# Order of the first loads in a one-token attention and MLP kernel: K ahead of the query weights, three small loads behind a GpSimd mask

## The chip, the cores and the metric

The kernel runs on one core of one Trainium2 chip. The metric is the device time of one execution in microseconds (us). The core has a matrix engine (TensorE, PE in the profile), VectorE (DVE), ScalarE (ACT), GpSimd (POOL) and SyncE (SP), which here only issues transfers. Sixteen DMA engines move the data between the memory (DRAM) and the on-chip SBUF. Transfers that SP issues form one queue (q1 in the profile); those that ScalarE issues form another (q10).

## What is computed

The reference works on one token with 1024 features (bfloat16) and adds three terms:

```python
x  = A_x                                   # (1, 1, 1024)
xn = layernorm(x)
# attention over the last W = 4096 positions of a cache, 32 query heads, 4 KV heads, head size 128
q  = xn @ wq                               # wq (1024, 4096)
p  = softmax(q @ k.T * 128 ** -0.5)        # k, v: (4 heads, 4096, 128)
a  = (p @ v) @ wo                          # wo (4096, 1024)
# MLP with a layernorm of its own
h  = gelu(layernorm(xn) @ w1 + b1)         # w1 (1024, 3584)
m  = h @ w2 + b2                           # w2 (3584, 1024)
out = x + a + m
```

All weights and the cache window together are 39.85 MB, and each byte is used once.

## The kernel before

The kernel is one instruction stream for each engine, written out by hand, with semaphores between them. There is no loop over tiles of an activation: the work is a row of stages, and each stage consumes one large transfer.

**Transfers.** SP issues everything large, in this order: the first half of wq (4 MB, line 157, called from `load_chunks`), the first half of K (2 MB, line 231, `load_k`), the second half of wq (4 MB), the second half of K (2 MB), and w1 (7 MB). These five go out at the start with no wait. SP then waits for VectorE's fourth transpose of K (`C["kt", 3]`), issues V (2 x 2 MB, line 311) into the room of K, waits for the last query matmul and issues w2 (4 MB and 3 MB) into the room of wq, waits for the last matmul with w1 and issues wo in four pieces (16, 11, 4 and 1 of its 32 chunks, line 318). In K and V one row of a transfer is 16 KB, in the halves of wq 32 KB.

**Small loads.** ScalarE issues three small loads as its first instructions: x (2 KB in 16 rows of 128 B, line 166, `row_load`, semaphore `s_x`), b2 (the same form, `s_b2`) and b1 (7 KB in 32 rows of 224 B, line 170, `s_b1`). It then waits for GpSimd to have zeroed `QBD` (line 178), zeroes three PSUM banks (lines 223 and 224) and later computes the square roots of the layernorms (line 251).

**Constants.** GpSimd builds masks and zeroed tiles from 0.81 us on: `onesb` (line 175), `identb` (memset in line 177, made an identity by the affine select in line 180), `QBD`, `YZ`, `XZ`, and more up to line 219.

**The stages.** (1) TensorE spreads x over 128 partitions (line 426, waits for `s_x`), VectorE makes the two layernorms and the transposed x (lines 244 to 277, ending in `XZ`, line 274). (2) TensorE multiplies with wq (64 matmuls of the `add` helper, line 430; a register loop waits on `s_feed`, which GpSimd raises when a half of wq has landed). (3) Meanwhile VectorE transposes K in four pieces (`turn_k`, line 284); the first three stand in its program in front of the query's transpose (line 292), the fourth behind the copies into `QBD` (line 303). (4) TensorE computes the scores (32 matmuls), VectorE the maximum, ScalarE the exponentials (line 344). (5) TensorE multiplies with w1 (56 matmuls), then probabilities with V (32 matmuls). (6) TensorE multiplies with w2 and wo in 11 rounds of 8 matmuls, then with the last 16 chunks of wo in small tiles (line 507); both halves of the result are copied (line 400) and stored (line 402).

Since the `add` helper records every matmul under line 430, its stages are told apart by their tiles: XZ with BIG is the query stage, QBD with KT the scores, YZ with BIG the w1 stage, KT with KV the product with V, GO with BIG the last stage.

Of the kernel before, what the change touches and what calls it, by code (L numbers as in the profile page):

```python
# [19 lines left out]
NQ = HQ * DH  # L20
W1_CHUNKS = [8]
WQ_CHUNKS = [4, 4]
# [29 lines left out]
def bass_parallel_sum__sliding_block_cached__mixer_channel_mlp__decode_kernel(  # L52
# [17 lines left out]
    pe, dve, act, pool, sp = nc.tensor, nc.vector, nc.scalar, nc.gpsimd, nc.sync  # L70

    def sems(name, n):
        return [nc.alloc_semaphore(f"{name}{i}") for i in range(n)]

    s_x, s_b1, s_b2, s_v, s_out = (nc.alloc_semaphore(n) for n in ("s_x", "s_b1", "s_b2", "s_v", "s_out"))
    s_w1 = sems("s_w1", len(W1_CHUNKS))
    s_wq = sems("s_wq", len(WQ_CHUNKS))
# [6 lines left out]
    POOL = Track(nc, "S_POOL")  # L84
# [4 lines left out]
    def sb(name, shape, d):  # L89
        return nc.alloc_sbuf_tensor(name, shape, d)  # L90

    f32, bf16 = dt.float32, dt.bfloat16
    identb = sb("identb", [128, 128], bf16)
# [11 lines left out]
    B1R = sb("B1R", [32, F // 32], bf16)  # L105
# [32 lines left out]
    WA, W1 = BIG[:, 0:KC * NQ], BIG[:, KC * NQ:KC * NQ + KC * F]  # L138
# [8 lines left out]
    wq_p = A_wq.rearrange("(p r) n -> p r n", r=KC)  # L147
# [5 lines left out]
    C = {}  # L153

    def load_chunks(dst, src, chunks, width, semaphores, c0=0):
        for j, n in enumerate(chunks):
            sp.dma_start(  # L157
                dst[:, c0 * width:(c0 + n) * width].rearrange("p (c n) -> p c n", c=n),
                src[:, c0:c0 + n, :],
            ).then_inc(semaphores[j], 16)  # L160
            c0 += n

    XB = XBRP[:, :].rearrange("p (a n) -> p a n", a=16)[:, :, 0:D // 16]

    def row_load(dst, src, semaphore):
        act.dma_start(dst, src.rearrange("o (a n) -> o a n", a=16)).then_inc(semaphore, 16)

    row_load(XB[0:1], A_x.rearrange("b s n -> (b s) n"), s_x)
    row_load(XB[1:2], B_b2.rearrange("(o n) -> o n", o=1), s_b2)
    act.dma_start(B1R[:, :], B_b1.rearrange("(p c) -> p c", p=32)).then_inc(s_b1, 16)  # L170

    def pool_wait():
        pool.wait_ge(POOL.sem, POOL.cnt)

# [44 lines left out]
    POOL.mark(pool.tensor_tensor(out=HALF[:, :], in0=HALF4[:, 0:2], in1=HALF4[:, 2:4], op=ALU.add))  # L219
    C["consts"] = POOL.cnt  # L220

    act.wait_ge(POOL.sem, C["QBD"])
    ACT.mark(act.activation(out=PS[:, 0:1024], in_=QBD[:, :], func=ACTF.Copy))
    ACT.mark(act.activation(out=bank(7), in_=QBD[:, 0:512], func=ACTF.Copy))
# [5 lines left out]
    def load_k(c):  # L230
        sp.dma_start(KV[:, c * 8192:(c + 1) * 8192], pairs(A_k_cache, c)).then_inc(s_k[c], 16)  # L231

    load_chunks(WA, wq_p, WQ_CHUNKS[:1], NQ, s_wq)
    load_k(0)
    load_chunks(WA, wq_p, WQ_CHUNKS[1:], NQ, s_wq[1:], WQ_CHUNKS[0])
    load_k(1)
    load_chunks(W1, w1_p, W1_CHUNKS, F, s_w1)

# [321 lines left out]
```

## Time and profile before

| what | value |
|---|---|
| median of 3 runs | 98.8 us (98.8 to 98.97) |
| the profiled execution's own time | 99.37 us |
| its span, first to last instruction | 97.4 us |
| around the span | 1.97 us |
| TensorE busy | 73.0 us (75%) |
| VectorE, ScalarE, GpSimd busy | 38.9, 11.2, 9.9 us |
| moved by DMA | 39.88 MB, mean 409 GB/s over the span |
| packets of SP's queue, share of 16 engines' span | 95.7% |
| granted TensorE clock, mean | 0.965 |

The profile is of one execution, whose time is 0.57 us above the median of the runs without a profile, so sums are made against it and carried over as differences. "Busy" counts compute instructions alone; a transfer's issue takes an engine's sequencer (SPq, ACTq) but is not counted as busy. The chain that ended last follows the last instruction back to what released it, step by step.

### The profile page before, as it was taken

How to read it: one execution, taken by the hardware profiler on the slowest of the kernel's cores; microseconds unless marked ns; L12 is line 12 of the kernel's file. 1: busy time of each engine (PE TensorE's matmuls, PEld its weight loads, DVE VectorE, ACT ScalarE, POOL GpSimd, SP SyncE). 2: the span in 40 equal slices, each digit the busy share in tenths (PEclk: the TensorE clock that was granted, in tenths of full speed). 3: DMA queues.
4: the chain of work that ended last, by engine and by line, in shares of the span. 5: the costliest groups of instructions: out<-in, count | busy, mean ns of one | idle time of the engine just before them, and what ended most of it. 6: DMA issues, size and time to landing. Idle time of an engine off the chain costs nothing.

```text
span 97.4 us, 1285 instructions
## 1 busy us (share of the span) xinstructions
PE 73.0 (75%) x354; PEld 30.4 (31%) x354; DVE 38.9 (40%) x54; ACT 11.2 (12%) x20; POOL 9.9 (10%) x27
## 2 busy tenths in 40 slices
PE   0004000099999986999979999799999999779992
PEld 0000000033444431333434444333343443334450
DVE  0002899899930799940293620050048000000001
ACT  0880000600000024000005200200000000000001
POOL 6999400000000000000000000000000000000000
PEclk9999999999999998557999999999999999999999
DMA  7599999999999998888999999999999999899890
GB/s 215 256 431 431 405 432 444 431 444 431 410 431 481 636 424 377 377 377 377 437 431 431 437 498 431 431 444 394 394 464 498 431 431 431 376 435 426 372 377 1
DMA packets 1989, 39.88 MB, mean 409 GB/s; under 512 B 322, under 2 KB 324, under 8 KB 452
## 3 DMA queue, kind: packets, MB, share of 16 engines
q1 hardware_dynamic: 1876, 39.85, 95.7%
q10 hardware_dynamic: 112, 0.01, 0.1%
q8 instruction: 1, 0.02, 0.1%
HBM read 39.86 MB, written 0.00 MB: 409 GB/s over the span
## 4 chain that ended last, share of the span: by engine, by line
DMA 80%; PE 14%; SPq 3%; issue 1%; DVE 0%
DMA BIG<-in_B_w_dram 47%; DMA BIG<-in_A_wo_dram 33%; PE PS L430 13%; SPq L231 1%; SPq L157 1%; SPq L318 1%; DVE Pb L400 0%; PE PS L507 0%
## 5 line engine op out<-in xcount | busy, mean ns | idle before, releaser
L430 PE MATMUL PS<-BIG,XZ 128*128 x64 | 16.5, 427 | 10.2 <-DVE B L277 10.2
L430 PE MATMUL PS<-BIG,GO 128*128 (+1 forms) x148 | 22.2, 337 | 1.4 <-POOLq L420 1.2
L284 DVE STREAM_TRANSPOSE KT<-KV 128x4096 bf16<-128x4096 bf16 x4 | 17.6, 4432 | 4.8 <-DMA KV<-in_A_k_cache_dram 4.8
L430 PEld LDWEIGHTS PS<-BIG,GO 128*128 (+1 forms) x148 | 9.9, 97 | 13.8 <-issue 6.4
L430 PEld LDWEIGHTS PS<-BIG,XZ 128*128 x64 | 6.9, 108 | 20.3 <-issue 14.3
L430 PE MATMUL PS<-BIG,YZ 128*128 x56 | 12.4, 380 | 0.6 <-DMA BIG<-in_B_w_dram 0.6
L430 PE MATMUL PS<-KT,QBD 128*128 x32 | 10.0, 491 | 1.0 <-ACT QBD L305 1.0
L430 PE MATMUL PS<-KV,KT 128*128 x32 | 8.3, 381 | 0.5
L400 DVE CAST Pb<-PS 64x256 bf16<-64x256 f32 x1 | 0.4, 417 | 20.4 <-PE PS L507 20.4
L430 PEld LDWEIGHTS PS<-BIG,YZ 128*128 x56 | 5.4, 96 | 7.6 <-issue 1.8
L426 PE MATMUL PS<-XBRP,onesb 1*128 1x512 bf16 x2 | 1.0, 616 | 8.1 <-DMA XBRP<-in_A_x_dram 8.1
L430 PEld LDWEIGHTS PS<-KT,QBD 128*128 x32 | 3.8, 120 | 7.2 <-issue 5.2
L244 DVE BATCH_NORM_STATS2 BN<-PS 128x6 f32<-128x512 f32 x2 | 1.3, 689 | 9.1 <-PE PS L426 9.1
L430 PEld LDWEIGHTS PS<-KV,KT 128*128 x32 | 3.1, 96 | 5.3 <-issue 3.8
L332 DVE TENSOR_REDUCE MX<-PS 128x1 f32<-128x1024 f32 x2 | 2.4, 1220 | 5.6 <-PE PS L430 5.6
L379 DVE SCALAR_TENSOR_TENSOR QBD<-PS,REC,HALF 32x256 f32<-32x256 f32 x2 | 0.9, 474 | 6.9 <-PE PS L430 6.8
L344 ACT ACTIVATE Pb<-PS,NMB 128x2048 bf16<-128x2048 f32 x1 | 2.0, 1968 | 13.8 <-DVE NMB L341 13.8
L348 DVE STREAM_TRANSPOSE KT<-Pb 128x2048 bf16<-128x2048 bf16 x1 | 2.3, 2311 | 2.1 <-ACT Pb L344 2.1
L353 DVE COPY HT<-PS 128x28 f32<-128x28 f32 x1 | 0.2, 210 | 6.4 <-PE PS L430 6.4
L400 ACT ACTIVATE Pb<-PS 64x256 bf16<-64x256 f32 x1 | 0.4, 381 | 20.1 <-PE PS L507 20.1
L426 PEld LDWEIGHTS PS<-XBRP,onesb 1*128 1x128 bf16 x2 | 0.1, 104 | 8.1 <-DMA XBRP<-in_A_x_dram 8.1
L290 ACT ACTIVATE Pb<-PS 128x512 bf16<-128x512 f32 x1 | 0.6, 597 | 16.6 <-PE PS L430 16.6
(77 smaller groups left out, 37.7 us busy)
## 6 DMA issues: line engine op xcount, KB each, us to landing
BIG<-in_A_wq_dram SPq DMA_DIRECT2D x2, 4096.0 KB, 18.8
BIG<-in_B_w_dram SPq DMA_DIRECT2D x1, 7168.0 KB, 46.0
KV<-in_A_k_cache_dram SPq DMA_DIRECT2D x2, 2048.0 KB, 23.1
KV<-in_A_v_cache_dram SPq DMA_DIRECT2D x2, 2048.0 KB, 13.6
BIG<-in_B_w_dram SPq DMA_DIRECT2D x1, 4096.0 KB, 24.8
BIG<-in_A_wo_dram SPq DMA_DIRECT2D x1, 4096.0 KB, 23.5
BIG<-in_B_w_dram SPq DMA_DIRECT2D x1, 3072.0 KB, 31.4
BIG<-in_A_wo_dram SPq DMA_DIRECT2D x1, 2816.0 KB, 29.8
```

The costliest lines, as they stand in the source:

```text
L157: sp.dma_start(dst[:, c0 * width:(c0 + n) * width].rearrange("p (c n) -> p c n", c=n), src[:, c0:c0 + n, :],).then_inc(semaphores[j], 16)
L231: sp.dma_start(KV[:, c * 8192:(c + 1) * 8192], pairs(A_k_cache, c)).then_inc(s_k[c], 16)
L244: DVE.mark(dve.bn_stats(out=BN[:, 12 * n + 6 * i:12 * n + 6 * i + 6], in_=src[:, 512 * i:512 * i + 512]))
L284: C["kt", n] = DVE.mark(dve.transpose(KT[:, n * 4096:(n + 1) * 4096], KV[:, n * 4096:(n + 1) * 4096]))
L318: sp.dma_start(BIG[:, first:first + n * D], wo_flat[:, c0 * D:(c0 + n) * D]).then_inc(s_wo[j], 16)
L332: C["mx"] = DVE.mark(dve.tensor_reduce(out=MX2[:, n:n + 1], in_=S[:, 1024 * n:1024 * n + 1024], axis=AX.X, op=ALU.max))
L344: C["exp"] = ACT.mark(act.activation(out=Pb[:, :], in_=S, func=ACTF.Exp, bias=NMB[:, 0:1], scale=SCALE, accum_out=SUMP[:, 0:1]))
L348: C["d_pt"] = DVE.mark(dve.transpose(PT[:, 0:2048], Pb[:, :]))
L379: DVE.mark(dve.scalar_tensor_tensor(out=ONM.rearrange("p (i c d) -> p i c d", i=2, c=PAIRS)[:, i], in0=PS[rows, 512:1024].rearrange("p (c ...
L400: track.mark(act.activation(out=to, in_=of, func=ACTF.Copy) if a else dve.tensor_copy(to, of))
L426: last = pe.matmul(bank(2 + i), lhsT=onesb[0:1, :], rhs=XB[0:1, 8 * i:8 * i + 8, :])
L430: return pe.matmul(to, lhsT=lhsT, rhs=rhs, start=False, stop=False, skip_group_check=True, **place)
```

## The change

SP issues the first half of K in front of the first half of wq; both halves of wq then follow each other, and the second half of K and w1 stay where they were. ScalarE's three small loads go out behind a new wait: ScalarE first waits until GpSimd has finished the identity mask `identb` (line 180). What ScalarE does after the loads is the same as before. No byte is added or removed, and no arithmetic changes.

```diff
@@ -165,10 +165,6 @@
     def row_load(dst, src, semaphore):
         act.dma_start(dst, src.rearrange("o (a n) -> o a n", a=16)).then_inc(semaphore, 16)
 
-    row_load(XB[0:1], A_x.rearrange("b s n -> (b s) n"), s_x)
-    row_load(XB[1:2], B_b2.rearrange("(o n) -> o n", o=1), s_b2)
-    act.dma_start(B1R[:, :], B_b1.rearrange("(p c) -> p c", p=32)).then_inc(s_b1, 16)
-
     def pool_wait():
         pool.wait_ge(POOL.sem, POOL.cnt)
 
@@ -219,6 +215,10 @@
     POOL.mark(pool.tensor_tensor(out=HALF[:, :], in0=HALF4[:, 0:2], in1=HALF4[:, 2:4], op=ALU.add))
     C["consts"] = POOL.cnt
 
+    act.wait_ge(POOL.sem, C["identb"])
+    row_load(XB[0:1], A_x.rearrange("b s n -> (b s) n"), s_x)
+    row_load(XB[1:2], B_b2.rearrange("(o n) -> o n", o=1), s_b2)
+    act.dma_start(B1R[:, :], B_b1.rearrange("(p c) -> p c", p=32)).then_inc(s_b1, 16)
     act.wait_ge(POOL.sem, C["QBD"])
     ACT.mark(act.activation(out=PS[:, 0:1024], in_=QBD[:, :], func=ACTF.Copy))
@@ -230,9 +230,8 @@
     def load_k(c):
         sp.dma_start(KV[:, c * 8192:(c + 1) * 8192], pairs(A_k_cache, c)).then_inc(s_k[c], 16)
 
-    load_chunks(WA, wq_p, WQ_CHUNKS[:1], NQ, s_wq)
     load_k(0)
-    load_chunks(WA, wq_p, WQ_CHUNKS[1:], NQ, s_wq[1:], WQ_CHUNKS[0])
+    load_chunks(WA, wq_p, WQ_CHUNKS, NQ, s_wq)
     load_k(1)
     load_chunks(W1, w1_p, W1_CHUNKS, F, s_w1)
```

## The prediction

> **What bounds the kernel now.** I read the page's chain of work that ended last first, then the chain in order of time, then the issues and the waits around the changed lines, and last the windows. The page's chain and its DMA line of the slices:
>
> ```profile
> DMA 80%; PE 14%; SPq 3%; issue 1%; DVE 0%
> DMA  7599999999999998888999999999999999899890
> ```
>
> Four fifths of the chain are transfers, and the DMA engines are full from the third slice (4.9 us) to the last but one. The chain in order of time:
>
> ```profile
> 0.81 0.40 SPq L157
> ...
> 3.28 45.97 DMA BIG<-in_B_w_dram
> ...
> 62.92 31.79 DMA BIG<-in_A_wo_dram
> 94.72 0.04 issue
> 94.76 0.62 PE PS L430 x16
> 95.38 0.02 issue
> 95.40 0.30 PE PS L507 x4
> ```
>
> The chain calls 12.46 us of TensorE and the issue of wo part of the way, but SP's queue isn't empty then: wo is issued at 62.08 and w2's second piece lands only at 75.9. In the trace's records of single packets, a DMA engine goes from one packet of SP's queue to the next without a gap over the whole run: 1.213 us for 32 KB, 0.611 us for 16 KB, from about 1.83 us to about 95.0. So **the end is the stream's start, plus a fixed number of bytes at a fixed rate, plus 2.7 us from the landing at 94.7 to the end of the span at 97.4**. At 16 x 32768 B per 1.213 us (432 GB/s) the 39.85 MB take 92.2 us of it. Only two things can move the end: a stream that starts otherwise, or compute so late that it outlasts the stream.
>
> The room that compute has stands in the waits of TensorE:
>
> ```profile
> PE PS L430 <- POOLq L420: 1.2, 1, 1.2
> PE PS L430 <- DMA BIG<-in_B_w_dram: 0.6, 1, 0.6
> PEld PS L430 <- DMA BIG<-in_A_wo_dram: 0.4, 1, 0.4
> ```
>
> In order of time: TensorE waits 0.57 us for w1 (to 49.61), 1.18 us for wo's first piece (to 85.92; GpSimd only passes its landing on), 0.43 us for wo's third piece (to 94.76). A further 0.2 us lies ahead of the scores, where VectorE is in its third K transpose until 36.80 while the query is ready at 36.51. A query that is late by up to 0.2 + 0.57 + 1.18 + 0.43 = 2.4 us costs nothing.
>
> **The change, part by part.** The issues that move, from the timeline:
>
> ```profile
> 0.81 0.58 ACTq L166 DMA_DIRECT2D XBRP<-in_A_x_dram  x1
> 0.81 0.40 SPq L157 DMA_DIRECT2D BIG<-in_A_wq_dram  x1
> 1.27 0.62 SPq L231 DMA_DIRECT2D KV<-in_A_k_cache_dram  x1
> 1.42 0.61 ACTq L166 DMA_DIRECT2D XBRP<-in_B_b_dram  x1
> 2.06 0.71 ACTq L170 DMA_DIRECT2D B1R<-in_B_b_dram  x1
> 2.27 0.29 POOL L180 TENSOR_SCALAR_AFFINE_SELECT identb<-identb 128x128 bf16<-128x128 bf16 x1 [0.23 <-POOL QBD L178]
> 8.08 0.12 PEld L426 LDWEIGHTS PS<-XBRP,onesb 1*128 1x128 bf16 x2 [8.08 <-DMA XBRP<-in_A_x_dram]
> ```
>
> *K first.* The stream begins 0.62 us behind the end of SP's first issue (1.21, first packet 1.83). That issue is now K's. The same form, issued after SP had idled 38 us (V's first, at 42.61), took 0.546 us; K's own two took 0.617 and 0.547 behind others. Against wq's 0.402 that is 0.14 to 0.22 later; I take 0.14, the row that also meets an idle queue. Against it stands that ScalarE no longer issues x in the same 0.4 us: wo's first piece, issued alone, took 0.328 instead of 0.402, and the store at the end had its first packet 0.48 us behind its issue instead of 0.62. If all of that were ScalarE's doing, 0.21 us would come back; these are smaller and plainer transfers, so I count 0.04. Sum: the stream starts 0.1 us later (bounds -0.07 to +0.22).
>
> *The stream's first packets.* The first 32 KB packet of most engines took 1.72 to 1.95 us instead of 1.213 (extremes 1.415 and 2.146): some 0.57 us of start-up. SP's issues in midstream (42.6 to 44.9) leave the packets at their fixed length, so it isn't the issuing that slows them. Nothing here shows a stream that starts with 16 KB packets. I take the same 0.57 in time, so no change; if half the packet halved or removed it, -0.29 to -0.57; if it grew to the worst engine's 0.93, +0.36. After the first two transfers the same 6.3 MB have passed in either order, so wq's second half (27.5), K's second (32.3), w1 (49.3) and all later ones move only with the start.
>
> *wq's first half lands later, K's earlier.* wq's lands where K's landed, at about 17.8 instead of 12.9; TensorE first touches it at 19.33, so 1.5 us are left, and 0.7 if x comes 0.8 us earlier. K's lands near 7.5 instead of 17.8, but VectorE starts its transposes at 18.80, behind the layernorm in its program: no gain. SP waits for nothing among its five issues, so nothing else on SP moves; GpSimd's program is untouched.
>
> *x, b2 and b1 wait.* The mask is ready at 2.27 + 0.29 = 2.56, so x is issued near 2.6 instead of 0.81, b2 at 3.2, b1 at 3.8 to 4.5. Before, x took 7.2 us from issue to landing. The packet records show why: on every engine three packets of wq went ahead of x's (6.04), and one more between x's data and its semaphore write (7.26 to 7.72). Two ends follow. If issue to landing stays 7.2, x lands near 9.8, 1.8 later. If the same number of packets goes ahead, but of K's 0.611 us each, then x, open to the engines at about 3.2 + 0.6, runs near 5.9, its semaphore write at 6.5 to 7.0, landing near 7.2: 0.8 earlier. The packets being the rows next to x, I take 7.2. Either end is inside the room: later by 1.8 leaves 0.6 of the 2.4; earlier by 0.8 starts the query stage near 18.5 and ends there, since K's second half still lands at 32.3 and VectorE is still in it until 36.8. Without this cover, 1.8 us late would cost 1.8.
>
> The Trainium skill ("DMA: Bandwidth & Descriptors", Queues, rings and completion order) says that a DMA engine takes turns between its queues at each packet. The alternation of x's data, one packet, x's semaphore write agrees; the three packets ahead of x's first don't follow from it, and by the rule alone x would run behind one K packet, near 4.4. The sum would be the same by either.
>
> *Queued behind the new wait on ScalarE:* the table load (1.28, before at 2.80, now near 4.5), the zeroing of three banks (1.03 + 0.58, done near 7.4 instead of 5.6), the second table load (done near 8.7). The first square root stands at 10.91, or 10.1 with x 0.8 earlier: 1.4 us of cover. Gone, it would delay the layernorm, which has the 2.4 again. b1 and b2 aren't read before 35.8.
>
> Sum: 99.37 + 0.1 = 99.47 for the profiled execution; as a difference on the median, 98.9.
>
> **The rivals.**
>
> *The start-up shrinks.* Smaller first packets, and no small loads among the first issues, fill the engines sooner: -0.29 to -0.57 against +0.1, so 98.3 to 98.6. For it: 0.57 us is nearly half a 32 KB packet, as if something waited for a first piece. Against: the engine that started last lost only 0.2, so the loss looks tied to time, not to a packet.
>
> *The start-up grows.* K's rows spread over two heads' regions, and its first packets all run as the slowest engine's did: +0.1 + 0.36, 99.1 to 99.3. Against it, K's packets later in the stream are as regular as the others (0.611 each).
>
> *x comes late and costs TensorE a clock step.* This is the slower mechanism with its own place, the query stage. The windows:
>
> ```profile
> 20.00:25.00 5.00, 5.00 (x14) 1.84 (x13) 5.00 (x2) 0.00 (x0) 0.00 (x0) 1.00 0.97 419
> 25.00:30.00 5.00, 5.00 (x25) 2.27 (x24) 2.56 (x1) 0.00 (x0) 0.00 (x0) 1.00 0.93 400
> 40.00:50.00 10.00, 9.43 (x33) 3.64 (x31) 4.38 (x3) 0.00 (x0) 0.00 (x0) 0.75 1.01 437
> ```
>
> The first query matmuls take 0.427 us each up to 24.4 and 0.213 from there, and the trace has a half-speed stretch of 6.83 us at 38.2. If steps come on a grid of half that, 3.41 us, its edges lie near 24.5 and 21.1. A start moved from 19.33 past 21.1, by 1.8, would step up 3.41 us later: eight more slow matmuls, 8 x 0.213 = 1.7. Late by 3.5 against room of 2.4: +1.1 and the 0.1, so 100.0. It decides only if x lands past 9.8, the late end above.
>
> The Trainium skill ("TensorE: Matmul & The Clock Gate", Part 1) gives a free-running window of 3413 ns after which a busy array is released from half clock; the two steps in this trace agree with that.
>
> *The change doesn't do what it says:* K's issue costs no more than wq's when it comes first, x lands as late as ever, and nothing moves: 98.8.
>
> **How the numbers follow.** The runs span 98.8 to 98.97, so 0.2% (0.2 us) is about what a measurement can tell. Forecast 52% (its own range 98.7 to 99.1; 0.38 of it within 0.2 us, 0.14 above); start-up shrinks 22%, faster; start-up grows 14%, slower; late x 7%, slower; no effect 5%, same. Faster 0.22; same 0.38 + 0.05 = 0.43; slower 0.14 + 0.14 + 0.07 = 0.35. The range takes in both start-up cases but for the outer tail, and leaves out late x: 98.4 to 99.4.
>
> **What would show it.** Right: the stream of packets still without gaps, SP's first issue 0.5 to 0.6 us long, wo's pieces landing 0 to 0.25 later, TensorE still waiting for wo's last pieces, x's spread in line 426 ahead of 8.08 and the scores starting at the same 39.0. Wrong in the start: the landing of wo's third piece (now 94.7) before 94.5 or after 95.1. Wrong in the cover: the last TensorE work no longer waits for wo, or a gap in SP's queue.

## The result, and the profile after

The changed kernel is slower: 99.38 us median (99.3 to 99.71) against 98.82 us (98.8 to 98.97), ratio 1.0061 (95% interval 1.0049 to 1.0072), that is 0.5 to 0.7 us. The forecast was 98.9 with little or no change; 99.38 lies just inside the range's upper end of 99.4, and well above the forecast's own 99.1.

The page of the changed kernel, its chain that ended last and its DMA line:

```profile
DMA 80%; PE 13%; SPq 4%; issue 1%; DVE 0%
DMA  4699999999999898888899999999999999898990
```

The bound is the same. Only the first slice differs clearly: 0.4 of the DMA engines busy instead of 0.7. The chain in order of time (start, length, what):

```profile
0.81 0.64 SPq L231
...
3.25 46.55 DMA BIG<-in_B_w_dram
...
63.93 32.03 DMA BIG<-in_A_wo_dram
95.97 0.04 issue
96.01 0.30 PE PS L506 x4
```

w1 lands at 49.79 instead of 49.25, wo's last piece at 95.97 instead of 95.36, and the span is 98.0 instead of 97.4. Everything behind the stream moves by 0.5 to 0.6, so the time was lost ahead of w1, and none was lost or won back behind it. The timeline of the first issues, and of x's use:

```profile
0.81 0.64 SPq L231 DMA_DIRECT2D KV<-in_A_k_cache_dram  x1
1.50 1.04 SPq L157 DMA_DIRECT2D BIG<-in_A_wq_dram  x2
2.59 0.59 ACTq L166 DMA_DIRECT2D XBRP<-in_A_x_dram  x1
8.60 1.03 PE L425 MATMUL PS<-XBRP,onesb 1*128 1x512 bf16 x2 [8.60 <-DMA XBRP<-in_A_x_dram]
```

SP's first issue takes 0.64 instead of 0.40, and in the trace's records of single packets the first packet follows at 2.23 instead of 1.83; averaged over the 16 engines, 2.43 instead of 1.99. Up to 8.5 us the packets then run 0.80 us per engine over their steady length instead of 0.66. So: 0.44 of later start and 0.14 of slower fill, together 0.58. The first packets of w1, a stream position that both kernels share, start at 32.36 instead of 31.78 on the mean: 0.58 again. The two parts hang together: in the changed kernel the twelve first packets that start at 2.2 to 2.4 take 1.2 to 1.65 us, and the four that start at 2.8 to 2.9 take 0.7 to 0.9. So the sum is firmer than its split.

TensorE's waits say that compute was no part of it:

```profile
PE PS L429 <- DMA BIG<-in_B_w_dram: 1.8, 1, 1.8
PE PS L429 <- POOLq L419: 1.2, 1, 1.2
```

x landed 0.5 us later than before, at 8.55, and TensorE still waits for w1 and for wo's first piece, for w1 longer than before, since in this execution its clock wasn't halved during the scores.

### The profile page after: what moved, and what is told of

It is laid out like the page before. It is cut to its first block, busy times and chain, and to the rows that moved or that the text cites. A ratio compares the mean times of both kernels' runs of the same rounds, so it can differ in the third digit from the quotient of the medians.

```text
span 98.0 us, 1274 instructions
## 1 busy us (share of the span) xinstructions
PE 70.2 (72%) x343; PEld 29.6 (30%) x354; DVE 38.9 (40%) x54; ACT 11.2 (11%) x20; POOL 9.9 (10%) x27
## 4 chain that ended last, share of the span: by engine, by line
DMA 80%; PE 13%; SPq 4%; issue 1%; DVE 0%
DMA BIG<-in_B_w_dram 47%; DMA BIG<-in_A_wo_dram 33%; PE PS L429 13%; SPq L231 1%; SPq L317 1%; SPq L157 1%; DVE Pb L399 0%; PE PS L506 0%
## 5 line engine op out<-in xcount | busy, mean ns | idle before, releaser
L429 PE MATMUL PS<-BIG,GO 128*128 (+1 forms) x137 | 21.6, 334 | 2.0 <-POOLq L419 1.2
L429 PE MATMUL PS<-KT,QBD 128*128 x32 | 8.0, 379 | 2.0 <-ACT QBD L304 1.1
L429 PEld LDWEIGHTS PS<-KT,QBD 128*128 x32 | 3.1, 96 | 6.9 <-issue 4.7
```

The lines of the kernel that those rows point to most:

```text
L429: return pe.matmul(to, lhsT=lhsT, rhs=rhs, start=False, stop=False, skip_group_check=True, **place)
```

## The experiments

Each run is compared with the kernel before on the same chip and in the same session (medians 98.91 and 98.92 there). "First packet" is the start on the earliest engine and "mean start" that over 16 engines; "fill" is what the large packets of the first 4 us took over their steady length, per engine (before: 1.83, 1.99 and 0.64 us). The "form" of a transfer is the pattern by which its rows go to the 128 partitions: in a plain one, row after row goes to partition after partition; in K's, two blocks of 64 rows, one for each head, are dealt to the partitions in turn. Rows are "dense" when each begins where the one before it ends.

### Which half of the change: K first, or the wait

The theories at this point: K's issue is longer (issue), 16 KB packets start a stream badly (packet), or the loads' wait disturbs the start (wait).

```diff
 # e1_k_first, against the kernel before
-    load_chunks(WA, wq_p, WQ_CHUNKS[:1], NQ, s_wq)
     load_k(0)
-    load_chunks(WA, wq_p, WQ_CHUNKS[1:], NQ, s_wq[1:], WQ_CHUNKS[0])
+    load_chunks(WA, wq_p, WQ_CHUNKS, NQ, s_wq)
```

> The order of SP alone is changed: K's first transfer ahead of wq's, the three small loads at once as before. Issue theory (K's first issue is longer, 0.637 against 0.402 us, and its packets begin 0.78 instead of 0.62 us behind it, because of the form of K's transfer): the stream starts 0.4 to 0.5 us later, 99.3 to 99.4 us. Packet theory (a stream that starts with 16 KB packets fills more slowly): also 99.3 to 99.4. Wait theory (the loads behind the mask disturb or no longer open the start): 98.8, as before.

Measured: 99.58, ratio 1.0060 (1.0040 to 1.0079). The timeline:

```profile
0.81 0.60 ACTq L166 DMA_DIRECT2D XBRP<-in_A_x_dram  x1
0.81 0.63 SPq L231 DMA_DIRECT2D KV<-in_A_k_cache_dram  x1
```

The issue is as long as in the changed kernel, the first packet later still, at 2.47 (mean 2.87), behind x's first, at 2.19; the fill is 0.55. x landed at 2.65, 5.4 us earlier than before, and it bought nothing.

```diff
 # e2_wait, against the kernel before: only the three loads move
+    act.wait_ge(POOL.sem, C["identb"])
     row_load(XB[0:1], ...)   # and b2, b1
```

> Only the wait is changed: the three small loads behind the identity mask, wq first as before. Issue theory and packet theory: 98.7 to 98.8, with SP's first issue at 0.33 to 0.40 us; x lands 0.5 us later or more, which the room of 2.4 us hides. Wait theory: 99.3 to 99.4.

Measured: 99.00, ratio 1.0002 (0.9981 to 1.0023). First issue 0.401 us, first packet at 1.84: ScalarE's issues beside it had cost SP nothing. x landed at 9.63, 1.6 later, at no cost. K first is the whole loss; the wait theory falls. With K first the wait may even win something: the transfers from wq's second half on land 0.83 us later than before in the profile of e1_k_first, 0.58 in that of the changed kernel. The runs' times don't tell the two apart (ratios 1.0060 and 1.0061).

### Packet, issue, or the rows themselves

```diff
 # e3_wq_16k: wq's first half as two transfers of 16 KB rows
-    load_chunks(WA, wq_p, WQ_CHUNKS[:1], NQ, s_wq)
+    load_chunks(WA, wq_p, [2, 2], NQ, [s_wq[0], s_wq[0]])
-    pool.wait_ge(s_wq[0], 16)
+    pool.wait_ge(s_wq[0], 32)
```

> The kernel before with wq's first half as two transfers of 2 MB in 16 KB rows, so that the stream starts with 16 KB packets of a plain transfer; loads at once. Issue theory: the first issue stays near 0.40 us, the stream starts as before, 98.8 (98.7 to 98.9). Packet theory: 99.2 to 99.4.

Measured: 98.91, ratio 0.9991 (0.9970 to 1.0013). The packet theory falls: first packet at 1.83, fill 0.63.

```diff
 # e4_k_plain: e1_k_first with one contiguous region as K's first transfer
-    load_k(0)
+    sp.dma_start(KV[:, 0:8192], A_k_cache[0, 0, SK - 2 * W:SK, :]
+                 .rearrange("(p i) d -> p (i d)", i=64)).then_inc(s_k[0], 16)
```

> K first as in e1_k_first, but its first transfer reads one contiguous 2 MB region of the cache (128 rows of 16 KB) instead of two heads interleaved; it reads other cache rows than the reference. Issue theory: first issue near 0.40 us instead of 0.64, first packets at 1.83, 98.8 to 98.9. Packet theory: 99.3 to 99.4 as in e1_k_first.

Measured: 99.38, ratio 1.0042 (1.0026 to 1.0058). The timeline:

```profile
0.81 0.41 SPq L233 DMA_DIRECT2D KV<-in_A_k_cache_dram  x1
```

Neither theory explains it. The issue is back at 0.405 us and the first packet at 1.84, as the issue theory said, and yet two thirds of the loss stay. The time is the one that the packet theory named, but e3_wq_16k had packets of the same size and lost nothing. The fill is now 0.89 us. So there is a second term, which goes with K's rows and not with their size. In e4 they lie end to end, while wq's 16 KB rows in e3 lie 64 KB apart. That gave the next pair, a dense theory against a tensor theory, with the form tested by itself.

```diff
 # e5_k_pitch: e4_k_plain, rows 64 KB apart
-    A_k_cache[0, 0, SK - 2 * W:SK, :].rearrange("(p i) d -> p (i d)", i=64)
+    A_k_cache[0, 0, SK - 8 * W:SK, :].rearrange("(p i) d -> p (i d)", i=256)[:, 0:8192]
 # e6_wq_dense: e3_wq_16k, first of its two transfers from rows end to end
+    sp.dma_start(WA[:, 0:2 * NQ], A_wq[0:256, :].rearrange("(p r) n -> p (r n)", r=2)).then_inc(s_wq[0], 16)
```

> As e4_k_plain (plain first transfer of 128 rows of 16 KB from K's cache), but its rows lie 64 KB apart, as wq's do, instead of end to end; it reads other cache rows than the reference. Dense theory (rows end to end fill the 16 engines more slowly at the start): 98.8 to 99.0, first packets back to the lengths of e3_wq_16k (1.0 to 1.4 us). Tensor theory (K's cache itself is slow to start, wherever its rows lie): 99.3 to 99.4 as in e4_k_plain.

> As e3_wq_16k (the stream starts with 16 KB packets of wq), but the first 2 MB are read end to end, so that other rows of wq reach each place than in the reference. Dense theory: 99.2 to 99.4. Tensor theory: 98.9, as e3_wq_16k.

Measured: e5 98.99, ratio 1.0016 (1.0002 to 1.0030); e6 99.36, ratio 1.0066 (1.0043 to 1.0089). The first 4 us of the four plain starts with 16 KB packets (stretch and length, busy us of TensorE, its weight loads, VectorE, ScalarE and GpSimd, then granted clock, DMA share and GB/s), first e3_wq_16k:

```profile
0.00:4.00 4.00, 0.00 (x0) 0.00 (x0) 0.00 (x0) 1.28 (x1) 3.17 (x14) 1.00 0.60 193
```

then e5_k_pitch:

```profile
0.00:4.00 4.00, 0.00 (x0) 0.00 (x0) 0.00 (x0) 1.30 (x2) 3.17 (x14) 1.00 0.58 197
```

then e4_k_plain:

```profile
0.00:4.00 4.00, 0.00 (x0) 0.00 (x0) 0.00 (x0) 1.14 (x1) 3.17 (x14) 1.00 0.54 139
```

and e6_wq_dense:

```profile
0.00:4.00 4.00, 0.00 (x0) 0.00 (x0) 0.00 (x0) 1.28 (x1) 3.17 (x13) 1.00 0.54 135
```

In these plain starts the rate goes by the spacing of the rows, not by the tensor: 193 and 197 with 64 KB between rows, 139 and 135 end to end, from wq and from K alike. The fills are 0.63 and 0.50 against 0.89 and 0.90, and against the kernel before the transfers from wq's second half on land within 0.1 of their old time in the first two and 0.35 to 0.4 later in the other two. Dense rows lose their time in the first packet or two; after those, nearly every packet is back at 0.611.

```diff
 # e9_wq_form: wq's first half, same row length and pitch, in K's interleaved form
-    load_chunks(WA, wq_p, WQ_CHUNKS[:1], NQ, s_wq)
+    sp.dma_start(WA[:, 0:4 * NQ],
+                 A_wq.rearrange("(g m r) n -> m g (r n)", g=2, r=KC)[:, :, 0:4 * NQ]).then_inc(s_wq[0], 16)
```

> The kernel before, its first transfer still wq's first half in 32 KB rows 64 KB apart, but taken in K's form: two halves of 64 rows interleaved over the partitions, so that wq's rows are permuted. Form theory (SP's issue of such a form is longer and its packets follow later): first issue 0.60 to 0.64 us, first packets from 2.2 to 2.5 on, 99.1 to 99.3. If the form is free: 98.9 with first packets at 1.83.

Measured: 99.74, ratio 1.0081 (1.0058 to 1.0104). The timeline:

```profile
0.81 0.60 ACTq L166 DMA_DIRECT2D XBRP<-in_A_x_dram  x1
0.81 0.63 SPq L233 DMA_DIRECT2D BIG<-in_A_wq_dram  x1
```

With wq's own bytes, the form alone makes the issue 0.63 and the first packet 2.47 (mean 2.69), at a fill of 0.62 as before. A stream that starts in this form pays it: the mean start is 0.70 later, and the transfers from wq's second half on land 0.66 later. The median lies above the 99.1 to 99.3 expected, and part of that has nothing to do with the stream: three of the six executions spent 1.8 to 2.0 us outside their span, the others 1.4, as 17 of 18 executions of the kernel before did here. The spans are 98.0 to 98.1 against 97.4 to 97.6. So the form costs some 0.6 to 0.7 us, less than the ratio's 0.8.

### Is the stream's start really the end?

```diff
 # e7_late_start, against the kernel before
+    sp.wait_ge(POOL.sem, C["QBD"])
     load_chunks(WA, wq_p, WQ_CHUNKS[:1], NQ, s_wq)
```

> The kernel before with one wait: SP's first issue waits for GpSimd's memset of QBD (2.04 us), so that the stream starts about 1.25 us later and x lands ahead of it (near 2.7). Stream theory: the whole delay is paid, 1.2 to 1.3 us, 100.0 to 100.2. If the query stage were part of the bound, x's earlier landing would give some of it back: below 99.8.

Measured: 100.31, ratio 1.0135 (1.0120 to 1.0150), or 1.2 to 1.5 us for an issue that moved by 1.25:

```profile
2.06 0.40 SPq L157 DMA_DIRECT2D BIG<-in_A_wq_dram  x1
```

The median is a little above the 100.2 named. x landed at 2.64 here, and nothing came back: the transfers from wq's second half on land 1.24 later on the mean. The stream's start is paid whole.

### How much room x has, and where it ends

```diff
 # e8_late_x, against e2_wait
-    act.wait_ge(POOL.sem, C["identb"])
+    act.wait_ge(POOL.sem, 17)      # the affine select of E4
```

> The order of before, the three small loads behind a much later GpSimd mark (the affine select of E4, 6.36 us), so that x is issued near 6.4 and lands near 12.4, 4.4 us later than before (e2_wait: 1.6 later at no cost). The stream starts as before. Room theory of the prediction (2.4 us; up to 3.6 where TensorE is spared its half-speed stretch): 99.7 to 100.9, with TensorE no longer waiting for wo's first piece. If the end hung on the stream alone, whatever x does: 98.8 to 98.9.

Measured: 101.09, ratio 1.0210 (1.0173 to 1.0247), for an x that landed at 12.89, 4.9 later. The median is above the 100.9 named. If each microsecond past the room cost one, the room would be 2.8 (2.4 to 3.1). That this lies near the prediction's 2.4 is chance, since the place is not the one that the prediction named. TensorE still waits for wo's first piece, against the expectation:

```profile
PE PS L430 <- POOLq L420: 0.5, 1, 0.5
```

The stretch from 46 to 50 us, whose last two columns are DMA share and GB/s, before and then in e8_late_x:

```profile
46.00:50.00 4.00, 3.43 (x17) 1.44 (x15) 1.79 (x2) 0.00 (x0) 0.00 (x0) 1.00 0.94 406
```

```profile
46.00:50.00 4.00, 3.37 (x15) 1.25 (x13) 0.86 (x1) 0.00 (x0) 0.00 (x0) 1.00 0.83 311
```

V's issue, from the timeline of e8_late_x:

```profile
46.89 1.20 SPq L311 DMA_DIRECT2D KV<-in_A_v_cache_dram  x2
```

V is issued behind VectorE's fourth transpose of K, at 46.89 instead of 42.61, and w1's last packets end at 48.5 to 48.95. V's first packets start from 48.50 on, on five of the engines only at 49.5 to 50.1, and take up to 1.6 us instead of 0.611. The queue ran dry, and the stream paid a second start-up: V landed 1.9 us later than before, at 60.88. What part of that is the gap, K's form or the dense rows, no run separates, nor how late V could be issued at no cost.

### A cheaper form for the same K, and two that told nothing

```diff
 # e10_k_heads, against the changed kernel; VectorE waits for 32 on s_k[0]
-    load_k(0)
+    for g in range(2):
+        sp.dma_start(KV[g:128:2, 0:8192],
+                     A_k_cache[0, g, SK - W:SK, :].rearrange("(m i) d -> m (i d)", m=64)).then_inc(s_k[0], 16)
```

> The changed kernel with K's first transfer issued as two plain ones, one for each head (64 rows of 16 KB end to end each), same data in the same places. Form theory: first issue near 0.40 us instead of 0.64, first packets at 1.84 instead of 2.23. Dense theory: the slow fill of e4_k_plain stays. Both together: 99.2 to 99.4, little or nothing better than the changed kernel. Form alone: 98.9 to 99.0.

Measured: 99.37, ratio 1.0043 (1.0022 to 1.0065). The time is as expected, the reasons aren't: an issue of 64 rows to every second partition takes 0.55 us, with the first packet at 2.14 (mean 2.47) and a fill of 0.53. It is a late start with a normal fill, not an early one with a slow fill. Its rows are dense all the same, and so are those of e1_k_first, whose fill is 0.55: dense rows filled more slowly only in the early plain starts of e4_k_plain and e6_wq_dense.

```diff
 # e6_wq_dense, first transfer: e13_near_rows, e14_near_engines
+    A_wq.rearrange("(e j r) n -> e j (r n)", e=16, j=32)[:, 0:8, :]
+    A_wq.rearrange("(j e r) n -> e j (r n)", j=8, r=2)[0:16]
```

> As e6_wq_dense, but the 128 rows of 16 KB are 16 blocks of 8 rows: rows end to end within a block, blocks 512 KB apart (other rows of wq reach each place than in the reference). If a slow fill comes from different engines reading close to one another: first packets short again (1.0 to 1.4 us), the fill as in e3_wq_16k. If it comes from consecutive rows of one engine lying end to end: the fill as in e6_wq_dense. The form is K's kind, so 0 to 0.4 us of issue come on top: 98.9 to 99.3, and 99.3 to 99.7.

> The counterpart of e13_near_rows: block e's 8 rows of 16 KB lie 1 MB apart, and the 16 blocks' rows lie end to end (other rows of wq reach each place than in the reference). If closeness between engines is what counts: the slow fill of e6_wq_dense or worse, 99.3 to 99.8. If the rows of one engine count: short first packets, 98.9 to 99.3.

Measured: 104.33, ratio 1.0535 (1.0503 to 1.0567), and 103.72, ratio 1.0476 (1.0441 to 1.0511), far outside both theories' numbers. The first transfer never came up to speed, as the window of e13_near_rows shows (last column GB/s; 446 over the same stretch before):

```profile
5.00:10.00 5.00, 0.00 (x0) 0.00 (x0) 3.22 (x7) 2.02 (x4) 4.79 (x9) 1.00 1.01 213
```

Its packets took about twice their length throughout. Something in these transfers has a cost that hides the one in question. Both split the source into 16 blocks of 8 rows, and both have wide gaps (512 KB between blocks in one, 1 MB between the rows of a block in the other); no run separates the two. Whether dense rows start slowly because different engines read close together or because one engine's rows adjoin is open.

None of these versions beats the kernel before.

## Why the prediction was wrong

**What held.** The bound: the stream's start plus fixed bytes (e7_late_start). The cover of x: 1.6 us late costs nothing (e2_wait), 5.4 us early gains nothing (e1_k_first). wq's second half, K's second half, w1 and the rest moved only with the start and its fill, 0.58 each on the mean. The remark that the loss of the first packets is tied to time and not to a packet held too: engines that start late have short first packets. Of its own signs, the one for a wrong start came true: wo's third piece landed at 95.22, past the 95.1 named.

**The step that failed: "the stream starts 0.1 us later (bounds -0.07 to +0.22)".** It measured 0.44 on the mean. The issue took 0.637 where V's 0.546 was taken, and K's own 0.617 was the better row. The larger miss in the first packet's 0.40 is the distance from the issue's end to the first packet, held at wq's 0.62: it was 0.78 in this form, and 1.03 with x issued beside it (e1, e9). A start-up was priced as an issue with a constant behind it; the form lengthens both, as e9_wq_form shows with wq's own bytes. The credit of 0.04 for ScalarE's silence was nothing with wq first (0.401, 1.84), while with K first the first packet comes at 2.23 instead of 2.47 (one profile each).

The time, 99.38, fell inside the range only because the range took in the rival that the start-up grows. That rival's +0.46 is near the measured 0.56 by chance: it put 0.1 on the start and 0.36 on the fill, and it was 0.44 and 0.14.

**"I take the same 0.57 in time, so no change."** The first packets before ran 0.62 over on the mean, not 0.57, and the fill up to 8.5 us rose by 0.14. The rival that the start-up grows blamed K's rows for being spread over two regions. In plain starts it is dense rows that cost, 0.25 (e4_k_plain against before), and rows 64 KB apart cost nothing (e5_k_pitch). Whether density is also behind the 0.14 of the changed kernel is open, since e1_k_first issues the same rows in the same form at a fill of 0.55, below that of the kernel before.

**x's landing, 7.2 forecast, 8.55 measured.** The step "if the same number of packets goes ahead" failed: of K's packets six went ahead of x's on eleven of the engines and seven or eight on the others, not three. On the eleven the bytes agree: 6 x 16 KB and 3 x 32 KB. Counted from when x could reach the engines (issue's end plus the 0.6 to 0.8 us of the first packets), the packet in progress and 64 KB more went ahead in before, e2, e3 and e8, and on those eleven; on most engines of e10 it was 80 KB. The miss cost nothing because the landing, 0.5 us later than before, was still inside the room. The Trainium skill's rule of turns at each packet ("DMA: Bandwidth & Descriptors", Queues, rings and completion order) speaks of packets of typically 9 to 17 descriptors (a descriptor is one order to move so many bytes). The prediction's 4.4 took each record of the trace, one row here, for a whole packet, which the page doesn't say; x ran at 6.74, and only the alternation behind it looks like turns.

**The room.** 2.4 us was added up from TensorE's waits alone. e8_late_x shows that SP's refill of the queue with V, behind VectorE, has a room of its own, and there the loss was. It decided nothing in the changed kernel, but it was missing from the sum.

**The clock rival** played no part. The edges fall elsewhere from one execution to another (the step up at 24.5 in before and after, at 23.9 in e2_wait, at 21.6 in e3_wq_16k), as the free-running window of the Trainium skill ("TensorE: Matmul & The Clock Gate", Part 1) has it, so a start past 21.1 would have been no fixed threshold.

## What to carry to other kernels

Where a gapless transfer stream is the bound, the order of transfers cost time in one place here, the first transfer, as long as the queue never ran dry: choose for it a plain form, with rows that lie apart (64 KB in the starts that lost nothing), and let awkward forms come later, where the queue in front hides their issue. What a transfer costs at the head of a queue can't be read from its cost in midstream: compare the packets' own starts, not the issue lengths. And when counting the room of a late input, follow it to every issue that refills the queue, not only to the engine that computes.

## What was not expected of the hardware

- The same 4 MB, same rows, same packets: interleaving two halves over the partitions moves the first packet from 1.83 to 2.47 and everything behind it by 0.66 us (e9_wq_form, ratio 1.0058 to 1.0104).
- In a plain first transfer, rows of 16 KB end to end fill the idle engines 0.25 to 0.4 us more slowly than rows 64 KB apart, from wq and from K's cache alike (e3 to e6); in a running stream they take 0.611 us each. The same dense rows in the later, interleaved starts of e1 and e10 showed no slow fill (0.55 and 0.53).
- A small load on the other queue waited for the packet in progress and 64 KB more, on some engines 80 KB, whether the packets were 16 or 32 KB: from the end of x's issue to its first packet 4.65 us in the kernel before, 4.0 in e2_wait, 3.6 in the changed kernel.
- A first transfer of 16 blocks of 8 rows ran at about half rate to its end (213 GB/s, half of its packets took 1.26 us or more instead of 0.611); why, no run here shows.
